# DeltaNet attention and a GELU MLP in one kernel: constants moved to VectorE's early pauses, the row selector moved ahead on GpSimd

## The chip, the cores and the metric

The kernel runs on one core of a Trainium2 chip. The metric is device time in microseconds (us). Before the change three runs took 254.40, 254.64 and 255.61 us; the median is 254.64 us.

## The reference

Two computations follow each other. The first is a recurrent attention over 4 batches and 8 heads, with 768 steps and vectors of 48 elements; the second is a two-layer MLP over the 3072 resulting rows of 384 elements, with 2048 hidden units.

```python
k_n = k / (np.linalg.norm(k, axis=-1, keepdims=True) + 1e-06)
state = zeros(B, H, D, D)
for t in range(S):
    y[:, :, t] = einsum('bhd,bhde->bhe', q[:, :, t], state)
    v_old = einsum('bhde,bhd->bhe', state, k_n[:, :, t])
    state += beta[:, :, t] * outer(k_n[:, :, t], v[:, :, t] - v_old)
...
x = y.transpose(0, 2, 1, 3).reshape(B * S, H * D)
h = x @ w_in
out = gelu_tanh(h) @ w_out
```

## The kernel before

The 768 steps are cut into 12 chunks of 64 (index `c`). Each chunk is handled as two units (index `u = 2c + x`), each with 8 groups of heads, so that a tile fills 128 partitions. For a chunk the work goes through these steps, whose names stand in the order table:

- `load` brings k, q and v by DMA; `sq`, `sum`, `pow`, `eps` and `inv` make the reciprocal norms of the keys (lines 495 to 503).
- `prep`: `kn` scales the keys with these norms and casts them to bf16 in the tile `tok` (line 531, or `knc`, line 524, for both units at once), `qb` casts the queries. `Tk`, `Tq` or `T` transpose both on TensorE (line 540), and the copies `kTk`, `kTq`, `kT` bring the result back to SBUF. `GD`, `GQ` or `G` (line 564) are the products of keys with keys and queries; `dn` copies out the first, `wq` the second through a mask (line 571).
- `leaf` solves blocks of 8 steps: `F` (line 633) collects the blocks with the selector `sel`, `lp` scales by beta, `x0` starts the solution (line 640), `L` (line 649) spreads the rows with the selector `rows`, and six pairs `xm`, `xa` (lines 655 and 658) do the substitution; `xb` multiplies by beta.
- `scale` and `invert` build the inverse of a 64 by 64 block: `xe` (lines 602 and 599), `KZ`, `kz`, `GM` (line 620), the masked copy `lw` (line 623), then `X1`, `A4`, `B4`, `A5`, `B5` with their copies `rt`, `bde`, `be` into the tiles `bd`.
- `chain` carries the state from chunk to chunk, and `mlp` does the two layers (`up`, line 824; `gelu`, line 828; `down`, line 835).

Which engine does what, and in which order, is written out by hand: the string `ORDER` lists every operation with its engine (`d` VectorE, `g` GpSimd, `a` ScalarE, `s` SyncE, otherwise TensorE, with the PSUM bank behind `@`). `Flow.order` makes one queue for each engine from it, and `Flow.emit` puts semaphore waits where an operation needs another's result. Each engine runs its queue strictly in that order, so an operation that waits holds up all behind it on its engine.

The first 50 us prepare chunks 0 to 2, the roots of this pipeline. Constants are made in this time too. The names that matter here are `two` (line 380, minus two times the template, used by `rt`), `wz` (line 355, zeros for filler matmuls), `ladj4.1` and `ladj5.1` (line 418, a part of the tiles `rl`), `first0` (line 400, the first column of the solution `xl`), `bdz1` (line 421, zeros of a tile `bd`), `triwq1` and `triwq4` (lines 343 and 411, the template copied into `wq`), `pad3` (line 403, zeros beside the keys), `low1` (line 396), and on GpSimd `rowz` and `rows1` (lines 381 and 382), a zeroed tile and a selection that turns it into the row selector `rows`. `betaN` (line 349) copies beta from PSUM to SBUF, and `mln`, `mwp`, `muq` (lines 372 to 376) are masks.

Of the kernel before, what the change touches and what calls it, by code (L numbers as in the profile page):

```python
# [15 lines left out]

ORDER = """
bdz3:d tmplz:g k0x1.10:a k1.01:s tmpl0:g tmpl1:g bdz5:d k0x1.00:a beta11:s blk1:g one:g pad2:g pad0:d pad5:d ident:g trilw0:d beta01:s beta10:a bdz4:d
ident2:g bdz0:g k0x1.01:s k0x1.11:a mmlw:d identf:d blk2:g k1.00:s beta00:a blk3:g k0x0.00:a k1.10:s half:g own:g triwq4:g trilw1:a k1.11:s sel:d
q0.10:s k0x0.10:a unit:d betaT1@0 triwq0:g q0.01:s mmuq:d mln0:g tabS:a bdz2:g sq.0b:a k2.00:s pad4:g mwp0:g betaN101:d k0x0.11:a betaT0@6 sum.0b:d  # L20
rowz:g q0.00:s betaN100:d mln1:g pow.0b:a q0.11:s eps.0b:d pad1:g inv.0b:d betaN001:d sq.1:a kn.1:g q2.11:s k0x0.01:a sum.1:d k2.10:s muq0:g Tk.1@1
muq1:g ladj4.0:a k2.01:s betaN011:d pow.1:a betaN110:d eps.1:g pad3:d k2.11:s inv.1:d triwq1:d betaN010:d low1:d kn.2:d v0.10:s kn.3:d qb.1:a Tk.2@7
v0.01:s qb.0:g Tk.3@5 kTk.2:d q2.01:s rows1:g Tq.1@4 sq.0a:a betaN111:d kTk.1:d q2.10:s kTq.1:d kTk.3:a sum.0a:d q2.00:s GD.3@4 betaH1:d pow.0a:a
Tq.0@7 sq.2:a eps.0a:d rpad0:g v1.00:s inv.0a:d GD.2@2 betaN000:d GD.1@0 dn.3:a kn.0:g betaL1:d q1.01:s betaH0:d betaS1@6 dn.2:a sum.2:d low2:g
q1.00:s dn.1:a Tk.0@4 first0:d F.1@2 kTq.0:d pow.2:a q1.10:s eps.2:g kTk.0:d trilw2:g q1.11:s GQ.1@0 lp.1:d GD.0@4 betaL0:d x0.1:d L.1@7 q3.01:s
dn.0:a two:d inv.2:d GQ.0@2 wz:d knc.2:g xm1.1:d qbc.2:a F.0@4 k3.00:s wq.0:d xa1.1:d q3.10:s betaS0@5 xm2.1:d xa2.1:d betaS3@2 w1.0:g lp.0:d k3.11:s
betaC0:a xm3.1:d ladj5.1:d L.0@3 triwq2:a ladj4.1:d T.5@4 v0.00:s x0.0:d wqa.1:a xm1.0:d first1:g xa1.0:d kT.5:a qb.3:g xa3.1:d xm2.0:d v0.11:s
xa2.0:d trilw3:g Tq.3@0 xm4.1:d xm3.0:d betaC1:a xa3.0:d qb.2:g xa4.1:d xm5.1:d xm4.0:d T.4@6 xa4.0:d xa5.1:d betaS2@1 xm5.0:d xm6.1:d kT.4:a xa6.1:d
xa5.0:d Tq.2@4 kTq.3:d xb.1:g xm6.0:d triwq5:g xa6.0:d betaC2:a xb.0:d G.5@6 w1.1:g kTq.2:a xe.1:d G.4@0 dn.4:a v2.11:s xe.0:d KZ.1@4 kz.1:a wq.4:d
mwp1:g dn.5:a GM.1@4 xec.1:d KZ.0@0 ladj5.0:a F.2@3 wqa.5:a betaC3:a lw.1:d kz.0:a lp.2:d bdz1:d L.2@3 k3.01:s GM.0@4 x0.2:d X10.1:g KZ.2@6 lw.0:d  # L30
KZ.3@0 kz.3:a X11.1:g kz.2:a xm1.2:d GM.3@0 xa1.2:d rpad1:g A4.1@2 X11.0:g lw.3:d X10.0:g rt4.1:d k3.10:s xm2.2:d A4.0@1 X11.3:g xa2.2:d v1.01:s
B4.1@2 xm3.2:d xa3.2:d rt4.0:d q3.11:s GQ.2@6 GM.2@4 vb.0:a xm4.2:d vb.1:g wq.2:d k4.11:s B4.0@1 bde40.1:a triwq3:g lw.2:d V.0@6 X10.3:g k4.01:s
bde41.1:a bde40.0:a k4.00:s wqb.1:g xa4.2:d A4.3@2 xm5.2:d bde41.0:a A5.1@0 k4.10:s rt4.3:d GQ.3@4 R.0:a rt5.1:d A5.0@1 X11.2:g B4.3@2 v1.10:s rt5.0:d
B5.1@0 bde40.3:a xa5.2:d q3.00:s B5.0@7 X10.2:g xm6.2:d fill115@1 xa6.2:d be50.1:d be50.0:a v1.11:s wq.3:d xb.2:g be51.1:a A4.2@3 sq.3:a w2.0:g
be51.0:d v2.01:s xe.4:d U.0@0 bde41.3:d KZ.4@4 Un.0:a w2.1:g rt4.2:d kz.4:a O.0@6 sum.3:d A5.3@4 On.0:a S.0@2 rt5.3:d GM.4@0 sq.4:a xe.5:d X.0@6
B4.2@7 lw.4:d Sn.0:a fill85@4 KZ.5@4 xT.0:a sum.4:d X11.4:g bde40.2:a up4.0@2 kz.5:d pow.3:g up0.0@0 bde41.2:a up1.0 X10.4:d tabG:a up2.0 up12.0@6
qbc.3:d up3.0 A5.2@4 up13.0 rt5.2:d gelu0.0:a up5.0 up6.0 GM.5@4 eps.3:d inv.3:d knc.3:d up7.0 up14.0 A4.4@0 lw.5:d up15.0 turn.7:s B5.2@1 gelu3.0:a
rt4.4:d up8.0@4 X11.5:g up9.0 gelu1.0:a B5.3@0 vbc.1:g down00.0@6 be50.3:d up10.0 be51.3:a X10.5:d pow.4:g be50.2:a up11.0 V.1@2 gelu2.0:a T.6@0
v2.00:s A4.5@7 kT.6:d v2.10:s be51.2:a K.1 down01.0 R.1:a rt4.5:d q5.00:s G.6@4 k5.10:s B4.5@7 dn.6:a B4.4@2 xi4.5:d U.1@0 bde40.4:a down02.0 k5.00:s
wq.6:d bdc40.5:g Un.1:a down03.0 k5.01:s bde41.4:d bdc41.5:g eps.4:g A5.5@1 k5.11:s Z0.0:d wqb.5:g S.1@4 Q.1@2 q4.11:s Sn.1:d G.7@6 O.1 vbc.2:g  # L40
q4.01:s A5.4@0 rt5.5:d On.1:a down10.0@5 inv.4:d q4.10:s dn.7:d kn.9:g down11.0 rt5.4:d q4.00:s wq.7:d F.3@1 q5.01:s B5.4@4 lp.3:d V.2@2 sq.5:a x0.3:d
v3.10:s L.3@1 B5.5@0 xm1.3:d X.1@6 be50.4:a v3.01:s be50.5:a xa1.3:d K.2 be51.5:a xm2.3:d down12.0 be51.4:a xa2.3:d q5.11:s xT.1:d R.2:a down13.0
xm3.3:d q5.10:s xa3.3:d xm4.3:d qbc.4:g up0.1@2 xa4.3:d Z1.0:a up12.1@6 xm5.3:d xa5.3:d up1.1 kn.8:g xm6.3:d sum.5:d turn.9:s U.2@4 up13.1 Un.2:a
up14.1 xa6.3:d pow.5:g xb.3:d up15.1 xec.3:d Q.2@0 gelu3.1:a S.2@4 turn.8:s O.2 up2.1 Sn.2:d On.2:a up3.1 up8.1@6 gelu0.1:a qb.11:d up9.1 KZ.6@0
eps.5:d KZ.7@4 inv.5:d kz.6:a up10.1 kn.11:d up11.1 kz.7:a up4.1@0 kn.10:g turn.11:s qb.10:a GM.6@2 gelu2.1:a G.9@4 lw.6:d up5.1 up6.1 dn.9:a up7.1
T.10@6 X11.6:g v3.11:s wq.9:d gelu1.1:a down10.1@7 kT.10:d k6.10:s GM.7@4 X10.6:d G.8@2 k6.00:s G.10@0 lw.7:d dn.8:a down11.1 v3.00:s dn.10:a F.4@6
X10.7:d k6.11:s wqa.10:a down12.1 X11.7:g lp.4:d wq.8:d k6.01:s A4.6@4 G.11@0 x0.4:d q6.00:s rt4.6:d L.4@5 dn.11:a A4.7@6 X.2@2 xm1.4:d v4.00:s
# [856 lines left out]
```

## Time and profile before

| | before |
|---|---|
| median of three runs | 254.64 us |
| profiled execution, its span | 254.7 us |
| TensorE busy | 226.0 us, 89% |
| VectorE busy | 185.8 us, 73% |
| ScalarE busy | 157.4 us, 62% |
| GpSimd busy | 130.1 us, 51% |
| chain that ended last: TensorE / VectorE | 73% / 15% |

The profiled execution has no time of its own beside its span; the span is 0.06 us from the median of the timed runs. In the views that follow, a row of the timeline gives the start in us from the span's beginning, the duration in us, the engine, the line of the kernel, the operation, what it writes and reads, and in square brackets how long the engine was idle before it and what released it. Several equal instructions in a row are merged (x2 and so on). A row of the chain gives start, duration, and the engine that the end of the program was waiting for at that time.

### The profile page before, as it was taken

What the parts mean: (1) busy time and instruction counts of PE and PEld (TensorE: products, weight loads), DVE (VectorE), ACT (ScalarE), POOL (GpSimd) and SP (SyncE); (2) the same over time, 40 slices, a digit from 0 to 9 for tenths busy, and PEclk for the clock granted to TensorE, in tenths of its full rate; (3) what the DMA queues carried; (4) which work ended last, traced back from release to release, by engine and by line L of the source; (5) the groups of instructions that cost most, each with busy time, mean ns of one, the idle gap of its engine ahead of it and who ended that gap; (6) DMA issues with size and microseconds to landing.
All of it is one profiled execution on the core that took longest, in us unless ns stands there. A gap on an engine that the chain in (4) does not pass through costs nothing.

```text
span 254.7 us, 12256 instructions
## 1 busy us (share of the span) xinstructions
PE 226.0 (89%) x5500; PEld 178.3 (70%) x5502; DVE 185.8 (73%) x445; ACT 157.4 (62%) x244; POOL 130.1 (51%) x159
## 2 busy tenths in 40 slices
...
GB/s 103 165 144 118 184 162 95 165 127 117 128 130 105 112 126 124 135 165 147 119 146 167 100 36 131 147 153 130 56 93 167 62 49 4 33 68 64 3 93 62
DMA packets 104532, 28.25 MB, mean 111 GB/s; under 512 B 98592, under 2 KB 103712, under 8 KB 104480
## 3 DMA queue, kind: packets, MB, share of 16 engines
...
q10 hardware_dynamic: 2400, 0.54, 1.1%
q14 instruction: 9, 0.07, 0.1%
HBM read 20.64 MB, written 4.72 MB: 100 GB/s over the span
## 4 chain that ended last, share of the span: by engine, by line
PE 73%; DVE 15%; ACT 4%; DMA 2%; ACTq 2%; issue 2%; SPq 1%; POOL 0%
PE ps L835 24%; PE ps L824 22%; PE ps L692 5%; PE ps L620 3%; PE ps L752 3%; PE ps L773 2%; DMA vraw<-in_v_dram 2%; PE ps L697 2%; PE ps L564 2%; DVE lw L623 2%; DVE xl L658 2%; PE ps L633 2%; PE ps L759 2%; DVE ps L655 2%; PE ps L609 1%
## 5 line engine op out<-in xcount | busy, mean ns | idle before, releaser
L824 PE MATMUL ps<-xT,W 128*128 128x256 bf16 x576 | 76.8, 277 | 0.4 <-DVE xl L658 0.4
L835 PE MATMUL ps<-W,gT 128*128 128x384 bf16 x384 | 72.7, 326 | 0.0
L828 ACT ACTIVATE gT<-ps 128x1024 bf16<-128x1024 f32 x48 | 48.4, 1022 | 26.4 <-PE ps L824 25.8
L824 PEld LDWEIGHTS ps<-xT,W 128*128 128x128 bf16 x576 | 52.2, 99 | 9.3 <-DVE xl L658 0.5
L835 PEld LDWEIGHTS ps<-W,gT 128*128 128x128 bf16 x384 | 34.0, 97 | 18.2
L682 POOL TENSOR_SCALAR_AFFINE_SELECT bd<-lw 64x512 bf16<-64x512 bf16 x34 | 22.6, 667 | 37.7 <-DVE lw L623 28.6
L704 DVE TENSOR_TENSOR rl<-ps,two 128x384 bf16<-128x384 f32 (+1 forms) x48 | 22.9, 484 | 9.7 <-PE ps L692 9.5
L623 DVE CAST_PREDICATED lw<-mlw,ps 128x832 bf16<-128x832 uint16 x24 | 24.3, 1018 | 6.8 <-PE ps L620 6.5
L499 POOL TENSOR_TENSOR nrm<-nrm,half 128x16 f32<-128x16 f32 x9 | 26.6, 2956 | 2.8 <-DVE nrm L497 2.7
L343 ACT ACTIVATE bd<-ps 32x256 bf16<-32x256 f32 (+1 forms) x40 | 16.8, 428 | 8.2 <-PE ps L692 4.4
L692 PEld LDWEIGHTS ps<-lw,bd 128*128 128x128 bf16 x384 | 15.5, 98 | 4.2 <-POOL bd L682 1.2
L692 PE MATMUL ps<-lw,bd 128*128 128x32 bf16 (+1 forms) x384 | 17.2, 183 | 1.2 <-POOL bd L682 1.1
L658 DVE TENSOR_TENSOR xl<-ps,xl 128x96 bf16<-128x96 f32 (+4 forms) x72 | 16.0, 228 | 2.0
L655 DVE TENSOR_TENSOR ps<-ps,xl 128x64 f32<-128x64 f32 (+5 forms) x72 | 15.6, 221 | 2.0 <-PE ps L649 0.5
L343 ACT ACTIVATE ob<-ps 128x384 f32<-128x384 f32 x17 | 8.3, 490 | 14.0 <-PE ps L835 14.0
L722 POOL COPY bd<-xi 64x256 f32<-64x256 f32 x20 | 8.0, 401 | 16.4 <-ACT xi L343 8.5
L540 PE MATMUL ps<-ident,tok 128*128 128x128 bf16 x80 | 7.8, 246 | 8.1 <-POOL tok L531 3.8
L531 POOL TENSOR_TENSOR tok<-kraw,nrm 128x384 bf16<-128x384 f32 x9 | 8.5, 945 | 12.7 <-DVE bsb L349 5.6
L349 ACT ACTIVATE kT<-ps 128x512 bf16<-128x512 f32 x18 | 10.4, 596 | 6.4 <-PE ps L609 6.4
L343 ACT ACTIVATE dn<-ps 128x512 bf16<-128x512 f32 x18 | 10.4, 593 | 5.3 <-PE ps L564 5.3
L620 PE MATMUL ps<-kT 48*64 48x56 bf16 (+1 forms) x768 | 11.1, 196 | 2.8 <-ACT kT L349 1.4
L599 POOL TENSOR_TENSOR zt<-xb,blk 128x2048 bf16<-128x2048 bf16 x3 | 10.9, 3642 | 4.1 <-DVE xb L669 3.9
...
## 6 DMA issues: line engine op xcount, KB each, us to landing
...
```

Of the source, the lines that this page charges most:

```text
L343: return e.activation(out, in_, ACT.Copy) if e is nc.scalar else e.tensor_copy(out, in_)
L499: if e is nc.scalar else e.tensor_tensor(nr[:, 1, hx], nr[:, 0, hx], half[:, hx], ALU.pow), reads=[nrn, "half"] + ["one"] * (c < ROOTS),
L620: ins = e.matmul(P(ps("GM"))[hf(a), o_ + c0:o_ + c1], kT[s][r, y, g, hf(a)], kT[s][r, z, g, C * a + c0:C * a + c1])
L623: A(("dve",), op("lw"), lambda e, P: e.copy_predicated(lw[m][:, :, 0:LW - LB], mlw[:, :, :].rearrange("p w t -> p (w t)")[:, 16:16 + LW - ...
L655: A(("dve",), f"xm{m}.{c}", lambda e, P, m=m, w=w, part=part: e.tensor_tensor(part(P), P(f"L.{c}")[:, off[m]:off[m] + 2 * H * w].rearrange ...
L658: A(("dve",), f"xa{m}.{c}", lambda e, P, m=m, part=part: e.tensor_tensor(xl[y][:, :, m + 1:LB], part(P), xl[y][:, :, m + 1:LB], ALU.add), ...
L682: A(("pool", "dve"), op(f"X1{a}"), lambda e, P, src=lw[m][hf(a), :, LW - C:LW], dst=bd[b_][hf(a), :, hf(a)], a=a: e.affine_select(out=dst, ...
L692: ins = e.matmul(P(name)[:, C * h + c0:C * h + c1], bd[b_][:, h, :], rhs[:, h, :])
L704: A(("dve",), op(f"rt{i}"), lambda e, P, i=i, c0=c0, c1=c1, r_=r_: e.tensor_tensor(r_[:, 0:H, c0:c1], P(ps(f"A{i}")).rearrange("p (h t) -> ...
L824: ins = e.matmul(P(ph)[:, 256 * f:256 * f + 256].rearrange("p (x t) -> p x t", x=2), W1[:, j, 128 * (i + f):128 * (i + f) + 128], x_[:, :, ...
L828: A(("act",), f"gelu{i // 4}.{c}", lambda e, P, i=i, ph=ph: e.activation(g_[:, i:i + 4, :], P(ph).rearrange("p (f t) -> p f t", f=4), ACT. ...
L835: ins = e.matmul(P(po)[:, 0:DM], g_[:, f, 128 * b:128 * b + 128], W2[:, f, :], start=(f == 0), stop=(f == FC - 1))
```

## The change

Only `ORDER` differs. No operation is added, removed or given to another engine, and the queues of TensorE, ScalarE and SyncE are the same. On VectorE nine constants move ahead. `two`, `wz`, `ladj5.1` and `ladj4.1` now come directly after `identf`, before `sel`; `first0` comes after `unit` (line 394), `bdz1` after `muq`'s first set, and `triwq1`, `pad3` and `low1` before the first norm sum, `sum.0b`. The reciprocal `inv.1` and both key casts `kn.2`, `kn.3` of chunk 1 go ahead of three `betaN` copies. On GpSimd `rowz` and `rows1` move to a place before the masks, and one of the two `triwq` copies (`triwq4`) goes to the old place of `rows1`, behind the query cast `qb.0`. These are two pieces of the table as it is now:

```
 blk3:g k0x0.00:a k1.10:s half:g own:g trilw1:a k1.11:s two:d wz:d
 ladj5.1:d ladj4.1:d sel:d q0.10:s k0x0.10:a unit:d first0:d betaT1@0 triwq0:g rowz:g rows1:g q0.01:s mmuq:d bdz1:d mln0:g
...
 k2.11:s inv.1:d kn.2:d v0.10:s kn.3:d qb.1:a Tk.2@7 v0.01:s qb.0:g triwq4:g Tk.3@5 betaN011:d betaN110:d betaN010:d kTk.2:d
```

VectorE's queue around the key casts of chunk 1 (`tok<-kraw,nrm`), which comes after the norm sum over 128x16:

```order
 L497 TENSOR_REDUCE nrm<-sq 128x16
+L503 RECIPROCAL nrm<-nrm 128x16
+L531 TENSOR_TENSOR tok<-kraw,nrm 128x8x48 x2
 L349 TENSOR_SCALAR bsb<-ps 64x2x4
 L349 TENSOR_SCALAR bsb<-ps 64x22x4
-L403 MEMSET tok 128x16x8
-L503 RECIPROCAL nrm<-nrm 128x16
-L343 COPY wq<-tmpl 128x512
 L349 TENSOR_SCALAR bsb<-ps 64x2x4
-L396 MEMSET low 128x1
-L531 TENSOR_TENSOR tok<-kraw,nrm 128x8x48 x2
```

The reciprocal and the two casts now stand directly behind the sum; the copy of `wq` and two sets have left this place, and three copies of beta now come behind the casts.

VectorE's queue in the leaf solutions of chunks 1 and 0, where the constants `ladj` (the tiles `rl_1`) stood between the pairs of one chunk and the start of the other:

```order
 L637 TENSOR_TENSOR lp<-ps,bsb 128x112 [waits s0]
 L655 TENSOR_TENSOR ps<-ps,xl 128x64 [waits s2]
-L418 TENSOR_SCALAR rl_1<-tmpl 128x8x32
-L418 TENSOR_SCALAR rl_1<-tmpl 128x8x16
 L640 SCALAR_TENSOR_TENSOR xl<-lp,unit 128x16x7 [waits s2]
 L655 TENSOR_TENSOR ps<-ps,xl 128x96 [waits s0,s2]
```

The two constants are gone from here; the start of chunk 0 (line 640) follows the product of line 655 directly.

GpSimd's queue from the constant `own` to the masks `mlw`:

```order
 L390 TENSOR_TENSOR own<-blk 128x64
-L411 COPY wq<-tmpl 128x256 x2
+L411 COPY wq<-tmpl 128x256
+L381 MEMSET rows 128x512
+L382 AFFINE_SELECT rows<-rows 128x1024
 L372 AFFINE_SELECT mlw<-mlw 64x64
 L421 MEMSET bd 128x512
 L403 MEMSET tok 128x16x8
 L374 AFFINE_SELECT mlw<-mlw 64x64
-L381 MEMSET rows 128x512
```

One of two copies has left this place, and the zeroing and the selection of `rows` have come in ahead of the first mask.

More of the change, by code (lines that the diff above doesn't have):

```diff
@@ L18 @@
 bdz3:d tmplz:g k0x1.10:a k1.01:s tmpl0:g tmpl1:g bdz5:d k0x1.00:a beta11:s blk1:g one:g pad2:g pad0:d pad5:d ident:g trilw0:d beta01:s beta10:a bdz4:d
-ident2:g bdz0:g k0x1.01:s k0x1.11:a mmlw:d identf:d blk2:g k1.00:s beta00:a blk3:g k0x0.00:a k1.10:s half:g own:g triwq4:g trilw1:a k1.11:s sel:d
-q0.10:s k0x0.10:a unit:d betaT1@0 triwq0:g q0.01:s mmuq:d mln0:g tabS:a bdz2:g sq.0b:a k2.00:s pad4:g mwp0:g betaN101:d k0x0.11:a betaT0@6 sum.0b:d
-rowz:g q0.00:s betaN100:d mln1:g pow.0b:a q0.11:s eps.0b:d pad1:g inv.0b:d betaN001:d sq.1:a kn.1:g q2.11:s k0x0.01:a sum.1:d k2.10:s muq0:g Tk.1@1
@@ L22 @@
[L22 to L45, printed above, removed]
@@ L46 @@
-T.10@6 X11.6:g v3.11:s wq.9:d gelu1.1:a down10.1@7 kT.10:d k6.10:s GM.7@4 X10.6:d G.8@2 k6.00:s G.10@0 lw.7:d dn.8:a down11.1 v3.00:s dn.10:a F.4@6
-X10.7:d k6.11:s wqa.10:a down12.1 X11.7:g lp.4:d wq.8:d k6.01:s A4.6@4 G.11@0 x0.4:d q6.00:s rt4.6:d L.4@5 dn.11:a A4.7@6 X.2@2 xm1.4:d v4.00:s
+ident2:g bdz0:g k0x1.01:s k0x1.11:a mmlw:d identf:d blk2:g k1.00:s beta00:a blk3:g k0x0.00:a k1.10:s half:g own:g trilw1:a k1.11:s two:d wz:d
+ladj5.1:d ladj4.1:d sel:d q0.10:s k0x0.10:a unit:d first0:d betaT1@0 triwq0:g rowz:g rows1:g q0.01:s mmuq:d bdz1:d mln0:g tabS:a bdz2:g sq.0b:a
@@ new lines @@
+k2.00:s pad4:g mwp0:g betaN101:d triwq1:d pad3:d low1:d k0x0.11:a betaT0@6 sum.0b:d q0.00:s betaN100:d mln1:g pow.0b:a q0.11:s eps.0b:d pad1:g
+inv.0b:d betaN001:d sq.1:a kn.1:g q2.11:s k0x0.01:a sum.1:d k2.10:s muq0:g Tk.1@1 muq1:g ladj4.0:a k2.01:s pow.1:a eps.1:g k2.11:s inv.1:d kn.2:d
+v0.10:s kn.3:d qb.1:a Tk.2@7 v0.01:s qb.0:g triwq4:g Tk.3@5 betaN011:d betaN110:d betaN010:d kTk.2:d q2.01:s Tq.1@4 sq.0a:a betaN111:d kTk.1:d q2.10:s
+kTq.1:d kTk.3:a sum.0a:d q2.00:s GD.3@4 betaH1:d pow.0a:a Tq.0@7 sq.2:a eps.0a:d rpad0:g v1.00:s inv.0a:d GD.2@2 betaN000:d GD.1@0 dn.3:a kn.0:g
@@ new lines @@
+betaL1:d q1.01:s betaH0:d betaS1@6 dn.2:a sum.2:d low2:g q1.00:s dn.1:a Tk.0@4 F.1@2 kTq.0:d pow.2:a q1.10:s eps.2:g kTk.0:d trilw2:g q1.11:s GQ.1@0
+lp.1:d GD.0@4 betaL0:d x0.1:d L.1@7 q3.01:s dn.0:a inv.2:d GQ.0@2 knc.2:g xm1.1:d qbc.2:a F.0@4 k3.00:s wq.0:d xa1.1:d q3.10:s betaS0@5 xm2.1:d
+xa2.1:d betaS3@2 w1.0:g lp.0:d k3.11:s betaC0:a xm3.1:d L.0@3 triwq2:a T.5@4 v0.00:s x0.0:d wqa.1:a xm1.0:d first1:g xa1.0:d kT.5:a qb.3:g xa3.1:d
+xm2.0:d v0.11:s xa2.0:d trilw3:g Tq.3@0 xm4.1:d xm3.0:d betaC1:a xa3.0:d qb.2:g xa4.1:d xm5.1:d xm4.0:d T.4@6 xa4.0:d xa5.1:d betaS2@1 xm5.0:d xm6.1:d
@@ new lines @@
+kT.4:a xa6.1:d xa5.0:d Tq.2@4 kTq.3:d xb.1:g xm6.0:d triwq5:g xa6.0:d betaC2:a xb.0:d G.5@6 w1.1:g kTq.2:a xe.1:d G.4@0 dn.4:a v2.11:s xe.0:d KZ.1@4
+kz.1:a wq.4:d mwp1:g dn.5:a GM.1@4 xec.1:d KZ.0@0 ladj5.0:a F.2@3 wqa.5:a betaC3:a lw.1:d kz.0:a lp.2:d L.2@3 k3.01:s GM.0@4 x0.2:d X10.1:g KZ.2@6
+lw.0:d KZ.3@0 kz.3:a X11.1:g kz.2:a xm1.2:d GM.3@0 xa1.2:d rpad1:g A4.1@2 X11.0:g lw.3:d X10.0:g rt4.1:d k3.10:s xm2.2:d A4.0@1 X11.3:g xa2.2:d
+v1.01:s B4.1@2 xm3.2:d xa3.2:d rt4.0:d q3.11:s GQ.2@6 GM.2@4 vb.0:a xm4.2:d vb.1:g wq.2:d k4.11:s B4.0@1 bde40.1:a triwq3:g lw.2:d V.0@6 X10.3:g
@@ new lines @@
+k4.01:s bde41.1:a bde40.0:a k4.00:s wqb.1:g xa4.2:d A4.3@2 xm5.2:d bde41.0:a A5.1@0 k4.10:s rt4.3:d GQ.3@4 R.0:a rt5.1:d A5.0@1 X11.2:g B4.3@2 v1.10:s
+rt5.0:d B5.1@0 bde40.3:a xa5.2:d q3.00:s B5.0@7 X10.2:g xm6.2:d fill115@1 xa6.2:d be50.1:d be50.0:a v1.11:s wq.3:d xb.2:g be51.1:a A4.2@3 sq.3:a
+w2.0:g be51.0:d v2.01:s xe.4:d U.0@0 bde41.3:d KZ.4@4 Un.0:a w2.1:g rt4.2:d kz.4:a O.0@6 sum.3:d A5.3@4 On.0:a S.0@2 rt5.3:d GM.4@0 sq.4:a xe.5:d
+X.0@6 B4.2@7 lw.4:d Sn.0:a fill85@4 KZ.5@4 xT.0:a sum.4:d X11.4:g bde40.2:a up4.0@2 kz.5:d pow.3:g up0.0@0 bde41.2:a up1.0 X10.4:d tabG:a up2.0
@@ new lines @@
+up12.0@6 qbc.3:d up3.0 A5.2@4 up13.0 rt5.2:d gelu0.0:a up5.0 up6.0 GM.5@4 eps.3:d inv.3:d knc.3:d up7.0 up14.0 A4.4@0 lw.5:d up15.0 turn.7:s B5.2@1
+gelu3.0:a rt4.4:d up8.0@4 X11.5:g up9.0 gelu1.0:a B5.3@0 vbc.1:g down00.0@6 be50.3:d up10.0 be51.3:a X10.5:d pow.4:g be50.2:a up11.0 V.1@2 gelu2.0:a
+T.6@0 v2.00:s A4.5@7 kT.6:d v2.10:s be51.2:a K.1 down01.0 R.1:a rt4.5:d q5.00:s G.6@4 k5.10:s B4.5@7 dn.6:a B4.4@2 xi4.5:d U.1@0 bde40.4:a down02.0
+k5.00:s wq.6:d bdc40.5:g Un.1:a down03.0 k5.01:s bde41.4:d bdc41.5:g eps.4:g A5.5@1 k5.11:s Z0.0:d wqb.5:g S.1@4 Q.1@2 q4.11:s Sn.1:d G.7@6 O.1
```

7 lines of the change are left out of this document (added).

## The prediction

> **What bounds the kernel now.** I read the busy time by stage first. Each row gives a stretch in us, its length, the busy us (and instruction count) of TensorE, its weight loads, VectorE, ScalarE and GpSimd, then the granted TensorE clock, the share of the DMA engines and GB/s.
>
> ```profile
> 30.00:40.00 10.00, 5.98 (x254) 5.17 (x254) 9.05 (x20) 5.39 (x11) 4.89 (x10) 0.65 0.92 150
> 60.00:100.00 40.00, 39.09 (x1153) 30.68 (x1150) 34.70 (x86) 31.04 (x51) 23.88 (x24) 1.00 0.78 123
> ```
>
> Up to about 48 us VectorE is the full engine (9.05 of 10 us here) and TensorE waits for it; from 60 us on TensorE is full (39.09 of 40). The change touches only the first part. So its worth is how much earlier VectorE hands the first chunks to TensorE, provided that TensorE's dense part then starts earlier by as much and runs as fast.
>
> Next I read VectorE's timeline where the chain of waits enters it for good.
>
> ```profile
> 9.00 0.55 DVE L497 TENSOR_REDUCE nrm<-sq 128x8 f32<-128x384 f32 x1 [1.40 <-ACT sq L495]
> ...
> 11.54 0.34 DVE L349 TENSOR_SCALAR bsb<-ps 64x8 f32<-64x8 f32 x2
> 11.97 0.17 DVE L403 MEMSET tok<- 128x128 f32 x1
> 12.14 0.25 DVE L503 RECIPROCAL nrm<-nrm 128x16 f32<-128x16 f32 x1
> 12.31 0.51 DVE L343 COPY wq<-tmpl 128x512 bf16<-128x512 bf16 x1
> 12.85 0.17 DVE L349 TENSOR_SCALAR bsb<-ps 64x8 f32<-64x8 f32 x1
> 13.06 1.96 DVE L531 TENSOR_TENSOR tok<-kraw,nrm 128x384 bf16<-128x384 f32 x1
> 13.09 0.06 DVE L396 MEMSET low<- 128x1 f32 x1
> 14.95 0.54 DVE L531 TENSOR_TENSOR tok<-kraw,nrm 128x384 bf16<-128x384 f32 x1
> 15.72 0.42 DVE L343 COPY kT<-ps 128x512 bf16<-128x512 bf16 x1 [0.23 <-PE ps L540]
> ```
>
> Two equal key casts take 1.96 and 0.54 us. GpSimd's rows of the same time say why:
>
> ```profile
> 12.17 0.50 POOL L343 CAST tok<-qraw 128x384 bf16<-128x384 f32 x1
> 12.63 2.05 POOL L382 TENSOR_SCALAR_AFFINE_SELECT rows<-rows 128x1024 bf16<-128x1024 bf16 x1
> ```
>
> The selection of `rows` runs to 14.68; the first cast is held until about then and ends at 15.02. So 1.96 - 0.54 = 1.42 us of the chain is a stall behind an instruction of another engine.
>
> **The change part by part.** I follow the delay of VectorE's work, minus meaning earlier.
>
> *Term A, the key casts.* `kn.2` follows the reciprocal, which ends at 12.39, and not at 13.06: -0.67. Without `rows1` beside it, its stall goes: -1.42. Together -2.09.
>
> *Term B, what is late next there.* The query cast on GpSimd (12.17 + 0.50 = 12.67) now lies beside `kn.2`, and behind it comes `triwq4`, whose length alone I take from a later equal copy:
>
> ```profile
> 28.82 0.39 POOL L411 COPY wq<-tmpl 128x256 f32<-128x256 f32 x1
> ```
>
> If the same kind of hold acts, `kn.2` waits until 12.67 (+0.28) and `kn.3` perhaps behind `triwq4` (+0.39): 0 to +0.67. I take +0.5, since the hold was seen in the rows above.
>
> *Term C, the beta copies.* Three stood in a wait (0.34 for two, 0.17); they now stand behind `kn.3`, 0.51 in all. The wait of 0.23 before the `kT` copy at 15.72 takes up part: +0.3, bounds +0.2 and +0.5.
>
> *Term D, the early pauses.* The constants go to the time before 9.00, where VectorE had idle time (1.40 us before the norm sum alone), so by their own durations they cost nothing. But `rows1` comes to this place too. The rows of the two engines there:
>
> ```profile
> 4.53 1.74 POOL L411 COPY wq<-tmpl 128x256 f32<-128x256 f32 x2
> 4.62 1.38 DVE L391 TENSOR_TENSOR sel<-ident,own 128x1024 bf16<-128x1024 bf16 x1 [1.22 <-POOL own L390]
> ```
>
> Two copies of 0.39 take 1.74 beside `sel`, so they hold each other here as well. `rows1` then starts about when `sel` ends (4.62 + 1.38 = 6.0, perhaps 6.4 with the four constants now ahead of `sel`) and ends 2.0 later, at 8.0 to 8.4. `first0`, a small cast, comes in this time. How a small cast fares beside a GpSimd instruction:
>
> ```profile
> 18.45 0.88 POOL L531 TENSOR_TENSOR tok<-kraw,nrm 128x384 bf16<-128x384 f32 x1 [3.69 <-DVE bsb L349]
> ...
> 18.56 0.80 DVE L447 CAST bhl<-bsb 128x16 bf16<-128x16 f32 x1
> ```
>
> It ended at 19.36, as the other did at 19.33. If `first0` is held likewise, behind it still come `muq`'s set, `bdz1`, a beta copy, `triwq1` (0.51), `pad3` (0.17) and `low1` (0.06), some 1.6 us as an estimate from these rows and the 0.48 of `bdz1` below. The norm sum would start at 9.6 to 10.0 instead of 9.00, or at 10.15 if the copy of `wq` is held once more. This delay goes on in full, because ScalarE's root and square for chunk 1 follow that sum in its queue. Below zero it can't go: the sum waits for ScalarE's square, which the change doesn't touch. So 0 to +1.15; I take +0.6, nearer to the hold, which two pairs of rows show.
>
> The Trainium skill, "SBUF — State Buffer", section "Who interferes with whom", states this as a rule: the two engines share one pair of ports, given to one instruction until it ends, and on VectorE it is needed by copies and casts in the two-port modes and by operations with two SBUF inputs beside a GpSimd instruction that reads SBUF. By that rule `rows1` only changes its victim, from `kn.2` to `first0`, and D is at its upper half; the rows above agree with it (19.36 beside 19.33).
>
> The sum up to here is -2.09 + 0.5 + 0.3 + 0.6 = -0.7.
>
> *Term E, the small constants between the chains.* The chain in order of time, around 22 to 25 us:
>
> ```profile
> 21.96 0.26 DVE wz L355
> ...
> 23.92 0.38 PE ps L649 x6
> 24.30 0.46 PE ps L540 x8
> ...
> 24.78 0.58 DVE xl L640
> ...
> 25.38 0.28 DVE ps L655
> ```
>
> `wz`, `two` and `first0` leave here, some 0.45 us, but TensorE's products `F.1`, `L.1`, `GQ.0`, `F.0` are also just in time here, so most of it turns into waiting: -0.1, bounds 0 and -0.4.
>
> *Term F, `ladj`.*
>
> ```profile
> 23.45 1.01 POOL L481 DMA_DIRECT2D W<-in_moe_w_in_dram x1
> ...
> 23.92 0.94 DVE L418 TENSOR_SCALAR rl<-tmpl 128x256 bf16<-128x256 bf16 x2
> 24.78 0.56 DVE L640 SCALAR_TENSOR_TENSOR xl<-lp,unit 128x112 bf16<-128x112 bf16 x1
> ```
>
> The two constants occupy VectorE for 0.94 and push the start of chunk 0's solution to 24.78, and that puts its first product at 25.38. Without them the start runs beside TensorE's `L.0` (23.92 to 24.30), and the product can begin at 24.3: -1.1. From there VectorE's substitutions follow each other to 29 us. ScalarE's copies of `dn` and `kT` and TensorE's `G` have gaps of half a microsecond there and might become the bound, so the low end is -0.5. I take -1.1.
>
> *`bdz1`.*
>
> ```profile
> 33.71 0.48 DVE L421 MEMSET bd<- 128x512 f32 x1
> ...
> 34.79 1.02 DVE L623 CAST_PREDICATED lw<-mlw,ps 128x832 bf16<-128x832 uint16 x1 [0.46 <-PE ps L620]
> ```
>
> VectorE idles 0.46 behind it, waiting for TensorE, so taking it out only lengthens the wait: 0.
>
> The sum is -0.7 - 0.1 - 1.1 = -1.9 us against a span of 254.7, that is 252.8. The span is 0.06 from the median of the runs shown, so the same number stands for the median. With all good ends the sum is -2.09 + 0 + 0.2 + 0 - 0.4 - 1.1 = -3.4 (251.3); with all bad ends -2.09 + 0.67 + 0.5 + 1.15 - 0.5 = -0.3 (254.4).
>
> **The rivals.** The noise to beat: a measurement of this kernel tells about 0.5% from no change, here 1.3 us, so faster means below 253.4 and slower above 255.9.
>
> *Rival 1: the early hold eats the gain.* D, B and C come out at their upper ends and F at about half: the chunk 1 casts end hardly earlier, and only 0.3 to 1.2 of the sum is left: 253.5 to 254.4, taken at 254.0, no measurable change. For it speak the 19.36 and 19.33 above; against it, that in the queue order `ladj` is gone whatever happens early. It also covers the case that the change does not do what it says, if GpSimd's hold merely moves.
>
> *Rivals 2 and 3: TensorE's clock at the start of its dense part.* The rows by microsecond, clock in the third column from the end:
>
> ```profile
> 48.00:49.00 1.00, 1.00 (x18) 1.00 (x15) 1.00 (x2) 1.00 (x3) 0.00 (x0) 0.50 1.26 190
> ...
> 53.00:54.00 1.00, 1.00 (x15) 0.83 (x14) 0.03 (x1) 0.22 (x1) 0.05 (x1) 0.80 1.31 204
> 54.00:55.00 1.00, 1.00 (x25) 0.73 (x26) 0.93 (x4) 0.81 (x1) 0.00 (x0) 1.00 0.74 112
> ```
>
> The MLP's first products, from 50.0 on, run at half clock until about 53.5, 3.5 us after their start; half of that is lost, 1.75. *Rival 2:* after the change the clock is already full when they start: 1.75 more are gained, 252.8 - 1.75 = 251.0. *Rival 3, the slower one:* they start 1.9 earlier, but a gap in TensorE's first microseconds (a wait for the weights or for the first gelu) keeps the clock at half. Each microsecond of half clock costs 0.5. The gain of 1.9 is used up once the stretch is 3.5 + 3.8 = 7.3 us long; at 10 us it costs 3.25, and the time is 252.8 + 3.25 = 256.0. Against it speaks that TensorE was busy 1.00 in each of these rows. If the stretch is only 6 us long, the time is 252.8 + 1.25 = 254.0, no change.
>
> The Trainium skill, "TensorE: Matmul & The Clock Gate", Part 1, states that the clock is raised after one busy window of about 3.4 us and that these windows run freely, unrelated to the program's start. By that rule half the lift's time is luck of the run, and the three runs' spread of 1.2 us fits it; no row here shows the windows' phase.
>
> **How the numbers follow.** The forecast, 252.8 with its own range 251.6 to 253.4, has 0.50. Rival 1 has 0.22 (254.0, same). Rival 2 has 0.13 (251.0, faster). Rival 3 has 0.07 (256.0, slower), and the short form of it 0.08 (254.0, same). Faster is 0.50 + 0.13 = 0.63, same 0.22 + 0.08 = 0.30, slower 0.07. The range reaches from 251.0, the middle of rival 2, to 254.8, past rival 1 and the short form: it leaves out half of rival 2 and all of the slower one, with a little over for the bounds, under 0.2.
>
> **What would show it right or wrong.** In the new profile `kn.2` (line 531 on VectorE) should take about 0.5 to 0.8 us, with the first `kT` copy near 15.0 instead of 15.72, and the first product of chunk 0's leaf near 23.5 instead of 25.38. D shows in the start of the first norm sum on VectorE: 9.0 if nothing holds it, 9.6 by my value, 10 or later for rival 1, with a small cast at line 400 of 1 us or more. The MLP's first product should start near 48.1; rivals 2 and 3 show as a granted clock of 1.00 or 0.50 there. I am wrong if the first `up` starts later than 49.5, or if it starts early and the last `down` does not end earlier.

## The result and the profile after

| | before | after |
|---|---|---|
| median (runs) | 254.33 us (22) | 252.53 us (22) |
| profiled execution: time, span | - , 254.7 us | 252.06, 250.2 us |
| TensorE / VectorE busy | 226.0 / 185.8 us | 223.8 / 185.4 us |

The ratio of the times is 0.9919, with a 95% interval of 0.9896 to 0.9942: the changed kernel is about 0.8% faster, 1.8 us by the medians. The ratio leaves out the slow ones among the runs, which in the changed kernel are five of the 22 (255.0 to 258.55 us, at a granted clock of 0.951 to 0.959 where the others have 0.966 to 0.977). In a later series the same two kernels have a ratio of 0.9963 (0.9926 to 0.9999), 0.7 us by the medians, so the size of the gain is less sure than the first interval says. The pair of profiles alone (4.5 us in the span) says too much. A profiled execution's time is its span and 1.8 us (252.06 to 250.2), so the one of before that stands above would be about 256.5 us, an estimate from these numbers, among the longer ones of that kernel. Profiled again, before has a span of 252.4 us and a time of 254.21.

VectorE's timeline of the changed kernel, at the places that the prediction named, from the small cast `first0` (line 400) to the first `kT` copy:

```profile
6.62 1.59 DVE L400 CAST xl<-unit 128x16 bf16<-128x16 f32 x1
...
9.22 0.54 DVE L497 TENSOR_REDUCE nrm<-sq 128x8 f32<-128x384 f32 x1
...
12.34 0.25 DVE L503 RECIPROCAL nrm<-nrm 128x16 f32<-128x16 f32 x1 [0.62 <-POOL nrm L501]
12.63 1.32 DVE L531 TENSOR_TENSOR tok<-kraw,nrm 128x384 bf16<-128x384 f32 x2
13.99 0.42 DVE L349 TENSOR_SCALAR bsb<-ps 64x8 f32<-64x8 f32 x3
14.44 0.42 DVE L343 COPY kT<-ps 128x512 bf16<-128x512 bf16 x1
```

GpSimd's timeline of the same kernel:

```profile
5.82 2.33 POOL L382 TENSOR_SCALAR_AFFINE_SELECT rows<-rows 128x1024 bf16<-128x1024 bf16 x1 [0.15 <-POOL rows L381]
...
12.38 0.50 POOL L343 CAST tok<-qraw 128x384 bf16<-128x384 f32 x1
12.82 0.72 POOL L411 COPY wq<-tmpl 128x256 f32<-128x256 f32 x1
```

Both casts together take 1.32 us, where they took 2.43 (13.06 to 15.49). The small cast `first0` takes 1.59 us where it took 0.18; it ends at 8.21, and `rows1` at 8.15. Yet the norm sum starts only 0.22 later than before. The copy `triwq4` takes 0.72 beside the casts, where a later equal one took 0.39.

VectorE at the leaf solution of chunk 0 (its start, line 640, and its first product, line 655):

```profile
22.59 0.33 DVE L640 SCALAR_TENSOR_TENSOR xl<-lp,unit 128x112 bf16<-128x112 bf16 x1
23.49 0.27 DVE L655 TENSOR_TENSOR ps<-ps,xl 128x96 f32<-128x96 f32 x1 [0.57 <-PE ps L540]
```

The product came 1.89 earlier than before (25.38), the very size of the forecast, but with a pause of 0.57 that the forecast had not counted. At 37.50 the lead is 1.90. There TensorE stops between the fourth and the fifth of eight equal products, for 0.98 us in which the profile shows nothing that it waits for:

```profile
36.31 0.39 PE L692 MATMUL ps<-rl,bd 128*128 128x64 bf16 x4
37.69 0.37 PE L692 MATMUL ps<-rl,bd 128*128 128x64 bf16 x4 [0.98 <-issue]
...
48.85 2.14 PE L824 MATMUL ps<-xT,W 128*128 128x256 bf16 x18
```

VectorE waits 0.76 us behind it, and the lead falls from 1.90 to about 1.04. So the MLP's first product starts at 48.85, 1.09 earlier than before and not 1.9. TensorE's clock then widens the distance between these two profiles to 2.76 at 54 us. Most of what is missing to 4.5 comes between 125 and 150 us (1.43), where before again has gained as much on the first profile of before; so it belongs to that run and not to the change. The rows by microsecond, clock in the third column from the end:

```profile
47.00:48.00 1.00, 1.00 (x18) 1.00 (x15) 1.00 (x2) 1.00 (x3) 0.00 (x0) 0.50 1.31 200
48.00:49.00 1.00, 0.64 (x22) 0.48 (x21) 1.00 (x3) 1.00 (x2) 0.66 (x1) 0.65 1.29 195
49.00:50.00 1.00, 1.00 (x11) 0.90 (x10) 1.00 (x4) 0.98 (x3) 0.92 (x2) 1.00 1.27 185
```

It is full from about 48.7 on, before the first MLP product, where in before it was half until 53.4. The first 18 products take 2.14 us in all.

### The profile page after: what moved, and what is told of

The parts are those of the page before. It is cut to its first block, busy times and chain, and to the rows that moved or that the text cites. A ratio compares the mean times of both kernels' runs of the same rounds, so it can differ in the third digit from the quotient of the medians.

```text
span 250.2 us, 12255 instructions
## 1 busy us (share of the span) xinstructions
PE 223.8 (89%) x5500; PEld 176.8 (71%) x5502; DVE 185.4 (74%) x445; ACT 157.2 (63%) x244; POOL 130.0 (52%) x159
## 3 DMA queue, kind: packets, MB, share of 16 engines
q1 hardware_dynamic: 99200, 23.79, 53.5%
## 4 chain that ended last, share of the span: by engine, by line
PE 74%; DVE 15%; POOL 4%; issue 2%; DMA 2%; ACT 1%; ACTq 0%; POOLq 0%
PE ps L835 26%; PE ps L824 21%; PE ps L692 5%; PE ps L564 3%; PE ps L752 3%; PE ps L620 2%; PE ps L633 2%; DVE lw L623 2%; PE ps L773 2%; DMA xT<-xo 2%; PE ps L697 2%; DVE xl L658 2%; PE ps L759 2%; DVE ps L655 1%; PE ps L795 1%
## 5 line engine op out<-in xcount | busy, mean ns | idle before, releaser
L824 PE MATMUL ps<-xT,W 128*128 128x256 bf16 x576 | 75.3, 273 | 0.6 <-DVE lw L623 0.4
L824 PEld LDWEIGHTS ps<-xT,W 128*128 128x128 bf16 x576 | 51.1, 97 | 9.0 <-DVE lw L623 0.7
L623 DVE CAST_PREDICATED lw<-mlw,ps 128x832 bf16<-128x832 uint16 x24 | 24.3, 1018 | 5.5 <-PE ps L620 5.3
```

The source lines that it names most:

```text
L623: A(("dve",), op("lw"), lambda e, P: e.copy_predicated(lw[m][:, :, 0:LW - LB], mlw[:, :, :].rearrange("p w t -> p (w t)")[:, 16:16 + LW - ...
L824: ins = e.matmul(P(ph)[:, 256 * f:256 * f + 256].rearrange("p (x t) -> p x t", x=2), W1[:, j, 128 * (i + f):128 * (i + f) + 128], x_[:, :, ...
```

## The experiments

Two theories stood against each other. *H*: the gain is the hold of GpSimd's selection on the key cast, which goes when `rows1` goes; with it the four constants ahead of chunk 0's leaf. *S*: the remaining moves (the casts ahead of the beta copies, `first0`, `bdz1` and three small ones into the early pauses) bring as much. The expectations, written before each run, use other letters in part: rival O is close to S, and the theory S of a later one is H. The table collects the starts, in us, of four places in each profile, and the time. Median times are compared only within a series, since before itself has 254.15 to 254.97 in the series below.

| kernel | norm sum | `kT` copy | leaf product | first `up` | median; ratio to before, 95% |
|---|---|---|---|---|---|
| before | 9.00 | 15.72 | 25.38 | 49.94 | 254.33 |
| before again | 9.00 | 15.74 | 25.38 | 49.91 | 254.21, one run |
| after | 9.22 | 14.44 | 23.49 | 48.85 | 252.53; 0.9919 (0.9896 to 0.9942) |
| after again | 9.22 | 14.52 | 23.31 | 47.85 | 252.78, one run |
| GpSimd part alone | 9.00 | 14.32 | 23.96 | 48.57 | 253.33; 0.9965 (0.9935 to 0.9995) |
| VectorE part alone | 9.00 | 15.76 | 24.80 | 49.51 | 254.71; 1.0007 (0.9967 to 1.0048) |
| four constants alone | 9.00 | 15.57 | 24.26 | 49.70 | 255.27, one run |
| after, `first0` late | 9.00 | 14.35 | 23.79 | 48.81 | 253.41, one run |
| after, three repairs | 8.99 | 13.91 | 22.70 | 47.88 | 253.15; 0.9937 (0.9904 to 0.9970) |
| after, fillers | 9.21 | 14.49 | 23.55 | 48.59 | 253.23; 0.9954 (0.9924 to 0.9983) |
| selector and four constants | 9.00 | 14.04 | 22.73 | 49.19 | 254.86; 0.9986 (0.9955 to 1.0018) |
| after, in that series | 9.22 | 14.56 | 23.52 | 48.42 | 254.23; 0.9963 (0.9926 to 0.9999) |
| repairs and fillers | 9.00 | 13.83 | 22.89 | 47.92 | 252.69; 0.9918 (0.9885 to 0.9952) |
| after, `bdz1` late | 9.00 | 14.27 | 22.93 | 47.53 | 251.58, one run |

### The GpSimd part alone

```diff
- half:g own:g triwq4:g trilw1:a
+ half:g own:g trilw1:a
- betaT1@0 triwq0:g q0.01:s
+ betaT1@0 triwq0:g rowz:g rows1:g q0.01:s
- v0.01:s qb.0:g Tk.3@5
+ v0.01:s qb.0:g triwq4:g Tk.3@5
```

(and `rowz`, `rows1` gone from their old places; VectorE's queue as before).

> GpSimd's part of the change alone (the row selector ahead of the masks, one wq copy in its old place); VectorE's queue as before. Theory H (the long key cast was held by the row selector, and its new place is what frees it): the two casts of line 531 end at 14.1 to 14.4 instead of 15.49, the first kT copy starts at 14.3 to 14.6 instead of 15.72, the first product of chunk 0's leaf at 24.1 to 24.3 instead of 25.38, time 1.0 to 1.3 us below before (ratio 0.995). Rival O (what counts is that VectorE has fewer constants between 12 and 25 us; the selector's place does not matter): kT copy at 15.5 to 15.7, time within 0.2 us of before.

VectorE's timeline of this kernel:

```profile
13.06 0.55 DVE L531 TENSOR_TENSOR tok<-kraw,nrm 128x384 bf16<-128x384 f32 x1
...
13.53 0.55 DVE L531 TENSOR_TENSOR tok<-kraw,nrm 128x384 bf16<-128x384 f32 x1
14.32 0.42 DVE L343 COPY kT<-ps 128x512 bf16<-128x512 bf16 x1 [0.24 <-PE ps L540]
```

The first cast starts when it did before, and takes 0.55 where it took 1.96. Nothing else on VectorE was touched, so the 1.42 us of stall were the selection's doing: H. The lead of 1.40 at the `kT` copy is 1.37 at the first `up`. By the ratio the kernel is faster, by 0.05 to 0.65%; by the medians of its series 0.8 us, a little less than the 1.0 to 1.3 expected.

### The VectorE part alone

```diff
- unit:d first0:d betaT1@0 triwq0:g rowz:g rows1:g q0.01:s
+ unit:d first0:d betaT1@0 triwq4:g triwq0:g q0.01:s
- mwp0:g betaN101:d
+ mwp0:g rowz:g betaN101:d
- qb.0:g triwq4:g Tk.3@5
+ qb.0:g Tk.3@5
- eps.0a:d rpad0:g
+ eps.0a:d rows1:g rpad0:g
```

(against the changed kernel; GpSimd's queue is again that of before).

> VectorE's part of the change alone (constants early, casts directly behind the reciprocal); GpSimd's queue as before, so the row selector runs at about 12.6 to 14.7 again. Theory H: one of the two casts is held to 14.7 or beyond, the pair ends at 15.1 to 15.6, the three beta copies come on top, the first kT copy starts at 15.7 to 16.1, the first product of chunk 0's leaf at 24.6 to 25.0 (25.38 before, 23.49 after), time 0.4 to 0.8 us below before. Rival O: the casts are done before the selector gets going, kT copy at 14.4, leaf product at 23.5, time as with the whole change, 2 us below before.

The two engines' timelines:

```profile
6.36 1.57 DVE L400 CAST xl<-unit 128x16 bf16<-128x16 f32 x1
...
12.42 2.86 DVE L531 TENSOR_TENSOR tok<-kraw,nrm 128x384 bf16<-128x384 f32 x2
...
15.76 0.42 DVE L343 COPY kT<-ps 128x512 bf16<-128x512 bf16 x1
```

```profile
7.36 0.51 POOL L381 MEMSET rows<- 128x512 f32 x1
...
12.63 2.32 POOL L382 TENSOR_SCALAR_AFFINE_SELECT rows<-rows 128x1024 bf16<-128x1024 bf16 x1
```

The casts start 0.64 earlier and end at 15.28, only 0.21 earlier: the pair takes 2.86, beside a selection of 2.32 to 14.95. The three copies of beta behind them use up the 0.21, and the `kT` copy is where it was. `first0` takes 1.57 here too, to 7.93, though no selection is beside it: GpSimd runs short masks and sets there, the last of them to 7.87. So it isn't shown that `rows1` is what holds `first0`. The time is that of before, where H had expected 0.4 to 0.8 less. Without the selection's move, VectorE's moves gain nothing up to the `kT` copy. At the leaf product they gain 0.58, but the four constants that H counts as its own are among them.

### Both kernels once more

> The kernel before, profiled once more. The early places repeat within 0.1 us (kT copy 15.72, leaf product 25.38, first product of the MLP 49.94). If the granted clock's steps are tied to the program, it rises at 53.5 again; if they run freely, the rise comes anywhere between 50 and 57, and the span moves by half of the difference.

> The changed kernel, profiled once more. The early places repeat (kT copy 14.44, leaf product 23.49). TensorE stood still for 0.98 us at 36.7 without a wait that the trace shows. If the program causes this, it stands at the same place again and the MLP's first product starts at 48.85; if it is luck of the run, it is gone or elsewhere and the product starts at 47.9 to 48.1. The clock's rise, at 48.6 there, repeats or moves as for the kernel before.

No edit; this asks which of the differences belong to the run. TensorE's timeline of before again, and of after again:

```profile
49.91 2.74 PE L824 MATMUL ps<-xT,W 128*128 128x256 bf16 x18
```

```profile
47.85 2.14 PE L824 MATMUL ps<-xT,W 128*128 128x256 bf16 x18 [0.88 <-ACT xT L343]
```

The early places repeat to 0.2 us (the leaf product of after again comes 0.18 earlier). The stop of 0.98 isn't there in after again, whose first `up` is 2.09 ahead of before: the forecast's lead, undiminished. In before again the first 18 products took 2.74 where the first profile showed 3.81, since the clock rose at about 51.2 instead of 53.4. So the time of the clock's rise, and whether TensorE stops long, are of the run. The place of the stop is not: the third profile of the changed kernel and five of other kernels have it between the same two products.

### The four constants alone

```diff
- identf:d blk2:g
+ identf:d two:d wz:d ladj5.1:d ladj4.1:d blk2:g
```

> The kernel before with only two, wz, ladj5.1 and ladj4.1 moved ahead of sel on VectorE. Theory H: the key cast is held as before (1.96 us, kT copy at 15.7), the first product of chunk 0's leaf comes at 24.7 to 24.9 instead of 25.38, because it then waits for TensorE's spread product as in the run of VectorE's part alone (24.80); the MLP's first product at 49.3 to 49.5. Rival (my prediction's term F): the whole 1.1 us is gained, the leaf product is at 24.3.

VectorE's timeline, first at the key casts and then at chunk 0's leaf:

```profile
12.78 0.55 DVE L531 TENSOR_TENSOR tok<-kraw,nrm 128x384 bf16<-128x384 f32 x1
...
13.25 2.28 DVE L531 TENSOR_TENSOR tok<-kraw,nrm 128x384 bf16<-128x384 f32 x1
...
24.26 0.27 DVE L655 TENSOR_TENSOR ps<-ps,xl 128x96 f32<-128x96 f32 x1 [0.15 <-PE ps L649]
24.72 0.39 DVE L658 TENSOR_TENSOR xl<-ps,xl 128x96 bf16<-128x96 f32 x2 [0.19 <-DVE ps L655]
```

The leaf product is 1.12 earlier, of which 0.15 was there at the `kT` copy. So the rival of this expectation, the prediction's term F, came true (24.3), and not the 24.7 to 24.9. The hold now falls on the second cast, since the first had begun at 12.78, ahead of the selection (12.86 to 15.20): it takes whichever is there. The single time (255.27) shows nothing; this profile has a stop of 1.55 us on TensorE at 32.61.

### `first0` back at its late place

```diff
- unit:d first0:d betaT1@0
+ unit:d betaT1@0
- F.1@2 kTq.0:d
+ F.1@2 first0:d kTq.0:d
```

> The changed kernel with the cast first0 back at its old place on VectorE. In the changed kernel it is held 1.59 us beside the row selector and the first norm sum starts at 9.22. If this hold is all that delays the sum, it starts at 9.00 here, the first kT copy at 14.2 to 14.3 (14.44 to 14.52) and chunk 0's leaf product 0.2 earlier, at 23.1 to 23.3. If another instruction takes the hold over (the copy of wq behind it), the sum stays at 9.2.

VectorE's timeline:

```profile
9.00 0.55 DVE L497 TENSOR_REDUCE nrm<-sq 128x8 f32<-128x384 f32 x1 [0.55 <-ACT sq L495]
...
12.43 1.44 DVE L531 TENSOR_TENSOR tok<-kraw,nrm 128x384 bf16<-128x384 f32 x2
```

Without the held cast the norm sum is back at 9.00, with 0.55 us to spare. So term D is 0.22. About 0.1 of it is lost again in the casts, which take 1.44 here. The leaf product came at 23.79 and not at 23.1 to 23.3: TensorE's products are slower in this run (`L.0` takes 0.48 where it took 0.38), and `L.0` ends only at 23.26.

### Three repairs

```diff
- k2.11:s inv.1:d kn.2:d
+ k2.11:s betaN011:d betaN110:d inv.1:d kn.2:d
- qb.0:g triwq4:g Tk.3@5 betaN011:d betaN110:d betaN010:d
+ qb.0:g Tk.3@5 betaN010:d
- kn.0:g betaL1:d
+ kn.0:g triwq4:g betaL1:d
```

(and `first0` late, as above).

> The changed kernel with three repairs: first0 back at its old place, triwq4 behind the key cast kn.0 on GpSimd, and two of the three beta copies back in the wait of 0.62 us ahead of the reciprocal. By theory H each gives back what it cost: 0.2, 0.25 and 0.25 us. Norm sum at 9.00, the two key casts in 1.1 us instead of 1.32 to 1.41, kT copy at 13.7 to 13.9, leaf product at 22.7 to 22.9, time 0.6 us below the changed kernel (ratio to before 0.989). Rival: from 14 us on ScalarE, the DMA of the keys and TensorE bind, the leaf product stays at 23.1 or later, and the time is that of the changed kernel.

VectorE's timeline:

```profile
12.42 1.26 DVE L531 TENSOR_TENSOR tok<-kraw,nrm 128x384 bf16<-128x384 f32 x2
...
13.91 0.42 DVE L343 COPY kT<-ps 128x512 bf16<-128x512 bf16 x1
```

The `kT` copy is 0.53 ahead of the changed kernel's and the leaf product 0.79. The casts still take 1.26, with the query cast alone beside them (two alone, in the first experiment, ran from 13.06 to 14.08). The times of the two kernels can't be told apart by their ratios to before; the 0.6 us expected are not shown.

### Fillers ahead of the MLP

```diff
- A4.2@3 sq.3:a
+ A4.2@3 fill10@0 fill11@1 sq.3:a
- KZ.4@4 Un.0:a
+ KZ.4@4 fill12@2 fill13@7 Un.0:a
- KZ.5@4 xT.0:a
+ KZ.5@4 fill14@0 fill15@1 xT.0:a
```

These add six products on zeros to the changed kernel, in pauses of TensorE.

> The changed kernel with six filler matmuls of zeros (128x512) in TensorE's waits ahead of the MLP's first product: two ahead of line 773, two ahead of line 795, two ahead of the first product of line 824. The output is unchanged. Theory C (part of a run's time is the stretch in which the clock is still half after the MLP starts): the clock is at 1.00 when the MLP's first product starts, the runs' spread shrinks and the median is 0.3 to 1.0 us below the changed kernel. Rival: the fillers come too late to raise the clock or hold up the chain, and the time is the same or 0.5 us longer.

The rows by microsecond:

```profile
47.00:48.00 1.00, 0.63 (x24) 0.43 (x22) 1.00 (x2) 1.00 (x3) 0.02 (x1) 1.00 1.30 199
48.00:49.00 1.00, 0.90 (x6) 0.38 (x5) 1.00 (x2) 1.00 (x3) 0.92 (x2) 1.00 1.27 186
```

The clock is full all through. In its half on the clock theory C came true: the mean granted clock of the twelve runs is 0.973 to 0.980 (median 0.979, against 0.972 in the changed kernel's 22), and they lie within 2.1 us (252.44 to 254.56). Yet the median isn't below the changed kernel's. What the fillers cost in return isn't shown. The changed kernel's first MLP products ran at full clock in its three profiles without fillers, too.

### Selector and four constants, against the whole change

This is before with the diffs of the GpSimd part and of the four constants, and nothing of S. The changed kernel and the next one ran in the same series.

> The kernel before with GpSimd's part of the change and only the four constants two, wz, ladj5.1 and ladj4.1 early on VectorE; the casts, the beta copies, first0, bdz1, triwq1, pad3 and low1 stay where they were. Theory S (the selector's place and these four carry all of the gain, the rest of the change is worth nothing): norm sum at 9.00, kT copy at 14.1 to 14.4, chunk 0's leaf product at 22.9 to 23.4, time as the changed kernel within 0.3 us. Rival (the casts ahead and the other constants count, as my term A's first half and term E had it): the kT copy comes 0.7 later than in the changed kernel, at 15.1, the leaf product at 24.1, time 0.8 us above it.

> The changed kernel timed in the same series: ratio to before 0.992, median 1.8 to 2.1 us below it. Its profile shows once more where TensorE stands still without a recorded wait; if these stops are luck of the run, they are at other places than 36.7 and 71.4, and the MLP's first product starts at 47.85 plus what they cost ahead of it.

VectorE's timeline of the first of the two:

```profile
13.25 0.75 DVE L531 TENSOR_TENSOR tok<-kraw,nrm 128x384 bf16<-128x384 f32 x1
14.04 0.42 DVE L343 COPY kT<-ps 128x512 bf16<-128x512 bf16 x1
...
22.73 0.27 DVE L655 TENSOR_TENSOR ps<-ps,xl 128x96 f32<-128x96 f32 x1
```

At both places it is ahead of the whole change (14.44 to 14.56 and 23.31 to 23.52 in three profiles). So in the early part S is worth less than nothing: about 0.4 at the `kT` copy and 0.7 at the leaf. Of the 0.4, 0.28 may be of the run: the copy of `wq` ahead of the casts takes 0.23 here and 0.51 in the GpSimd part alone, and the query cast beside it started later here, after a wait of 0.20 for its DMA.

But its time is not shown to be below that of before, nor to be that of the changed kernel, as H had it: the medians are 0.6 us apart, and the intervals overlap. The clock is a part of this. Eight of its twelve runs have a mean granted clock of 0.966 or less, of the changed kernel's twelve only three, of before's 26 ten. The runs above that have medians of 253.95 (four runs), 253.73 (nine) and 254.59 us (sixteen); four are too few to settle it, and why the clock was lower isn't shown. Its one profile is of a run of 256.73 us, with a stop of 1.35 us at 46.66 and half clock until 52.3. Against the first profile of before it is 2.26 ahead at 38 us, 0.91 at 54 and 1.14 behind at 125, after stops of 0.96 and 0.48 us at 102.75 and 107.38. The changed kernel's profile of this series stops at the same two places (1.25 and 0.59). So the early lead can be lost later, in the dense part of TensorE.

The changed kernel itself had been expected at a ratio of 0.992, 1.8 to 2.1 us below before; it came at 0.9963, 0.7 us below. Its stop is at the old place again (0.72 us, to 37.46).

### Repairs and fillers together

The diffs of the three repairs and of the fillers, on the changed kernel.

> The changed kernel with the three repairs (first0 late, triwq4 behind kn.0, two beta copies ahead of the reciprocal) and the six filler matmuls together. By theory H and C: kT copy at 13.9, leaf product at 22.7, clock at 1.00 when the MLP's first product starts, median 0.5 us below the changed kernel and a spread of 2 us or less. Rival: the dense part of TensorE absorbs what is gained ahead of it, and the median is that of the changed kernel.

The rows by microsecond:

```profile
47.00:48.00 1.00, 0.68 (x3) 0.20 (x4) 1.00 (x3) 1.00 (x3) 0.66 (x1) 1.00 1.32 203
48.00:49.00 1.00, 1.00 (x10) 0.90 (x11) 1.00 (x4) 0.98 (x3) 0.95 (x1) 1.00 1.36 214
```

The first `up` is at 47.92 at full clock, and the median is 1.5 us below that of the changed kernel in the same series. It beats before by ratio (0.9885 to 0.9952); against the changed kernel the intervals overlap.

### One instruction fewer ahead of the leaf

The pause of 0.57 ahead of the leaf product was open: its only producer on TensorE, `L.0`, had ended at 22.97, the product began at 23.49. In the two kernels with the four constants ahead and `bdz1` at its old place (the four constants alone, and with the selector) it began 0.1 us after `L.0`, and a gap of 0.2 stood one instruction later.

```diff
- mmuq:d bdz1:d mln0:g
+ mmuq:d mln0:g
- kz.0:a lp.2:d L.2@3
+ kz.0:a lp.2:d bdz1:d L.2@3
```

> The changed kernel with one constant (bdz1) back at its old place behind lp.2, so that VectorE has one instruction fewer ahead of chunk 0's first leaf product. In the changed kernel that product starts 0.5 us after the end of L.0, its only producer on TensorE (22.97, product at 23.49); with the four constants alone it starts 0.1 us after it (24.16, product at 24.26), and the next instruction then has a gap of 0.19 ahead of it. Theory P (a stall that belongs to the position in VectorE's queue, as when the next instructions are not there yet): the product starts within 0.15 us of L.0's end and the gap of 0.1 to 0.4 us moves to the line 658 behind it. Theory W (a wait for TensorE, whose products of T.5 behind L.0 end at 23.42): nothing of that sort changes, and the product again starts about 0.5 us after L.0's end. Time: about that of the changed kernel by either.

VectorE's timeline, and TensorE's:

```profile
22.41 0.48 DVE L640 SCALAR_TENSOR_TENSOR xl<-lp,unit 128x112 bf16<-128x112 bf16 x1
22.93 0.27 DVE L655 TENSOR_TENSOR ps<-ps,xl 128x96 f32<-128x96 f32 x1
23.35 0.39 DVE L658 TENSOR_TENSOR xl<-ps,xl 128x96 bf16<-128x96 f32 x2 [0.15 <-DVE ps L655]
```

```profile
22.42 0.38 PE L649 MATMUL ps<-lp,rows 128*128 128x96 bf16 x6 [0.18 <-DVE lp L637]
```

`L.0` ends at 22.80 and the product starts at 22.93; the gap, now 0.15, has moved to the instruction behind it, which has the same number in VectorE's queue as the product had. This number is the 64th instruction that the trace records for VectorE. In the eight profiles in which the product has it, the product starts 0.51 to 0.52 us after the end of `L.0`; in the three in which the next instruction has it, that one starts 0.55 to 0.56 after it. In the other three VectorE gets there 1.0 us or more after `L.0`, and nothing waits.

The end of `T.5`, theory W, stands just ahead of the stalled instruction in most of these profiles. The kernel with `first0` late tells the two apart, since its `T.5` is slow:

```profile
22.78 0.48 PE L649 MATMUL ps<-lp,rows 128*128 128x96 bf16 x6
23.10 1.44 PE L540 MATMUL ps<-ident,tok 128*128 128x128 bf16 x12
```

```profile
23.79 0.27 DVE L655 TENSOR_TENSOR ps<-ps,xl 128x96 f32<-128x96 f32 x1 [0.90 <-PE ps L649]
```

The first eight of the twelve products are `T.5`. They end at 24.11, and VectorE's product started at 23.79. So the stall belongs to a place in the queue, and the products of `T.5`, which most of the profiles name, aren't its cause. What is missing there (the next instructions themselves, perhaps) isn't shown. The norm sum is at 9.00 with `first0` still early and long (1.60, to 7.96): VectorE has 0.29 us to spare there without the 0.48 of `bdz1`. The one run took 251.58 us.

## Why the prediction was right, and where its steps were not

The forecast of 252.8 us and the measured 252.53 agree, and so does the lead where VectorE is the bound: 1.89 at the leaf product, for the 1.9 of the sum. Some of this is luck. The 254.7 from which the 1.9 was taken is the span of a long run (about 256.5 us in time), and only by chance also the median; and in the later series the gain was 0.7 us and not 1.8. The steps behind the sum did not all hold.

- **A, the key casts.** Right: the GpSimd part alone removes the stall of 1.42, and the VectorE part alone shows that the earlier start is worth nothing at the `kT` copy while the selection stays behind it.
- **B and C.** Right in kind, B a little too high. The second cast ends at 13.95; 0.22 of that is D. From the reciprocal's end in before (12.39) to 13.73 are 1.34 us, and two unheld casts take 1.02 (13.06 to 14.08 in the GpSimd part alone), so B is 0.32 and not 0.5. From the casts' end to the `kT` copy are 0.49 (13.95 to 14.44) instead of 0.23 (15.49 to 15.72), so C is 0.26, near the 0.3.
- **D, the early pauses.** This is the term that was mis-sized: 0.22 in place of 0.6. `first0` did become long, and in the changed kernel it ends with `rows1`, as the rule of the Trainium skill has it ("SBUF — State Buffer", "Who interferes with whom": 8.21 beside 8.15). But it is as long where the selection is elsewhere (1.57 in the VectorE part alone), so its cause stays open. The pause of 1.40 took up most of it: what stands behind `first0` took 1.0 (8.21 to 9.22), where the working had 1.6. A to D thus gave 1.28 at the `kT` copy, not 0.7, and the copy came at 14.44 where the prediction said near 15.0.
- **E and F, the constants ahead of the leaf.** By themselves the two are nearly right: 1.12 with the four constants alone (0.15 of it from the `kT` copy), and 1.23 on top of the GpSimd part (23.96 to 22.73, 0.28 of it from there); that is 0.97 and 0.95 net, for the 1.2 forecast. In the whole change E and F together gave 0.6 (1.89 less 1.28) and not 1.2, because VectorE's stall of 0.57 now stood ahead of the product. The step that failed is that the product can begin when the start and `L.0` are done. The errors of A to D (0.6 too little, most of it D) and of E and F (0.6 too much) cancelled, which is luck.
- **The clock.** Rival 2 came in the profiles, and only there. In the three of the changed kernel the first 18 products took 2.14 us, against 3.81 and 2.74 in before. But the median granted clock of all the runs is 0.972 in the changed kernel and 0.971 to 0.973 in three series of before, so nothing shows the gain of the typical run to be the clock's. The stated 3.5 us at half clock were those of one long run; in another it was about 1.3 (49.91 to 51.2). The Trainium skill's "TensorE: Matmul & The Clock Gate", Part 1, has the windows run freely; the rise at 53.4 and 51.2 in two runs of one program agrees.
- **Rivals 1 and 3.** The early delay of rival 1 is there at `first0`, but far too small. Rival 3 was not seen in the three profiles of the changed kernel.
- **What I did not see** is TensorE's unexplained stop, which in the first profile took 0.86 of the lead, and VectorE's stall ahead of the leaf product. The first `up` was told near 48.1; it came at 48.85, 47.85 and 48.42.
